# Token mixing's second layer by seven products of half blocks, in four of eight batch elements of a fused attention and mixer kernel

## The chip, the cores and the metric

One core of a Trainium2 chip runs the whole program. The metric is the device time of one execution in microseconds (us), the median of several. All data are 32-bit floats.

## What is computed

For each of 8 batch elements: normalised attention of 12 heads over 448 positions of 64 channels, which gives x of 448 by 768, and then one mixer block on x. Cut to what matters here:

```python
h = np.maximum(xt @ w_tok1, 0.0) @ w_tok2      # xt: 768 x 448, w_tok1: 448 x 256, w_tok2: 256 x 448
u = x + h.transpose(0, 2, 1)                   # token mixing
h2 = np.maximum(u @ w_ch1, 0.0) @ w_ch2        # channel mixing: 768 -> 1536 -> 768
out = u + h2
```

The change concerns the second product of the first of these lines, in each element a matrix of 768 x 256 times one of 256 x 448, whose result is added to x.

## The kernel before

The kernel keeps x and then u of an element as six tiles of 128 channels by 448 positions, `st["uT", b][:, cc]`. The 256 hidden rows of token mixing lie in two tiles `h1` (one for each half of the 256, called jc), each 128 partitions by 768 channels. `tok1` (lines 843 to 877) makes them in two halves of 384 channels (h = 0 and 1), and `tok1_out` (lines 879 to 884) evicts each half with a Relu on ScalarE.

`tok2(b, cc)` (lines 886 to 895) is the second layer for one tile of channels: two matmuls with 448 columns, one for each half of the 256, add up in one PSUM bank (`m_tile`), and VectorE adds the bank to `uT` (line 894). It runs six times per element. After the two tiles t and t + 3, `moving_sums(b, t)` (lines 902 to 914) forms four sums T1 to T4 of quarters of u, two on VectorE and, from the third element on, two on GpSimd.

Channel mixing already uses fewer products than the plain way: `ch1` (line 997) by seven products of half blocks, three times per element, and `ch2` (line 1065) by 15 forms with tables of additions. Both use banks of `ps_M`, of which there are two. Scores of attention and some smaller things use the four banks of `ps_S`. `ch1`'s products i = 0 and 4 are evicted by a ScalarE copy, the others by VectorE (line 1015). Products i = 0, 1 and 5 read u, i = 2, 3, 4 and 6 read T2, T3, T1 and T4 of `moving_sums`.

Attention runs one element ahead, so the attention of element b + 1 lies in between the mixer work of element b. From the third element on (b = 2 to 6) `big_step` makes large blocks of attention and `place` (lines 638 to 655) puts them at written-out places among the mixer items: the first block stands directly behind the last `tok2` and ahead of the first `ch1`. A block brings `beside` items, put directly after it, and `between` items, spread over the mixer items up to the next block. For the first block `beside` is: two scalings of q and k (line 1507), two transposes into `qkT` (line 436, two instructions each), and two additions to the sums of exponentials (line 500).

Every engine runs its instructions in the order in which the program issues them; a list of items with costs (`us(n, cols)`) decides that order, and the costs have no other effect than on order. At the end of an element four finished tiles are transposed into `turned` and the last two are left for the start of the next element, among the items of token mixing (line 1103). SyncE issues nearly all DMAs, among them the weights of channel mixing (`load_units`, up to 7 units of 384 KB ahead) and the q and k of later heads (`loads`), which wait until the tile they overwrite has been transposed.

`raw_pool` has five tiles for the loading of weights, not used any more from the fourth element on. `x_pool` has two tiles that hold the transposed x of an element's two halves. `r_pool` holds scratch tiles r1, r2, r3 and r5 for `ch1` and `ch2`.

Of the kernel before, what the change touches and what calls it, by code (L numbers as in the profile page):

```python
# [8 lines left out]
F32 = mybir.dt.float32  # L9
# [74 lines left out]
def whole(ctx, tc, shifted, pre, q, k, v, g_q, g_k, moe_w_tok1, moe_w_tok2, moe_w_ch1, moe_w_ch2, out):  # L84
# [121 lines left out]
    def raw_tile():  # L206
        return raw_pool.tile([P, WCOLS, 2], U32, name="raw")
# [427 lines left out]
        between += [item(group_sums, t, k) for k in (5, 6)] + loads(n + 3)  # L635
        return [], (6.2, second_block), beside, between

    def place(units, blocks, at):

        res, i, rest = [], 0, []  # L640
        for j, (ahead, block, beside, between) in list(zip(at, blocks)) + [(len(units), ([], None, [], []))]:
            n, done = j - i, 0
            for m in range(n):
                if m == n - 1 and block:
                    res += ahead
                res.append(units[i + m])
                upto = -(-len(rest) * (m + 1) // n)
                res += rest[done:upto]
                done = upto
            if not n:  # L650
                res += rest + ahead
            i, rest = j, between
            if block:
                res += [block] + beside
        return res

# [186 lines left out]
    def tok1(b, jc, h):  # L843

        def main(start, stop):
            for c in range(NM):
                nc.tensor.matmul(  # L847
                    out=st["t1", h][jc][:, 0:HC], lhsT=w1_sb[:, c, jc * P:(jc + 1) * P],
                    rhs=st["x", b, h][:, :, c, :], start=start and c == 0, stop=stop and c == NM - 1)

        def rest(h, starts):
            for i in range(NJ):
                rows = slice(i * D, (i + 1) * D)
                nc.tensor.matmul(  # L854
                    out=st["t1", h][i][:, 0:HC], lhsT=w1_sb[rows, NM, i * P:(i + 1) * P],
                    rhs=st["x", b, h][rows, :, NM, :], start=starts[i], stop=not starts[i])

        alone, first = b > 0 and not shifted, jc == 0
        if first and not (alone and h):
            st["t1", h] = [m_tile() for i in range(NJ)]  # L860
        if not alone:
            main(first, not first)
            if first:
                rest(h, (False, True))
            tok1_out(jc, h)
            return
        if h == 0:
            main(True, False)
            return
        if first:  # L870
            st["t1", h] = [s_tile("t1_ps") for i in range(NJ)]
            rest(0, (False, False))
            rest(1, (True, True))
            for i in range(NJ):
                tok1_out(i, 0)
        main(False, True)
        tok1_out(jc, h)

    def tok1_out(jc, h):

        if h == 0:
            st["h1", jc] = h1_pool.tile([P, C], F32, name="h1", tag="h1")
        nc.scalar.activation(
            out=st["h1", jc][:, h * HC:(h + 1) * HC], in_=st["t1", h][jc][:, 0:HC], func=AF.Relu)

    def tok2(b, cc):
        ps = m_tile()
# [258 lines left out]
    def middle_items(b):  # L1146

        items = []
        for t in range(KC):
            items += [(us(NJ, S), lambda cc=cc: tok2(b, cc)) for cc in (t, KC + t)]  # L1150
            if b:
                items.append((0.0, lambda t=t: moving_sums(b, t)))
        if b == 0:
            return items, [(us(4, S), lambda n=n: first_stage(n)) for n in range(len(stages))]
        items += [(us(6, HS), lambda mp=mp, i=i: ch1(b, mp, i)) for mp in range(KF // 2) for i in range(7)]
        if b == 1:
            double = [(us(6, S), lambda mt=mt, h=h: plain_2(b, mt, h)) for mt in order_2 for h in range(2)]
        else:
            double = [(us(4, HS), lambda f=f, x=x: ch2(b, f, x)) for f in range(NF9) for x in range(2)]
        mixing.update(fn for _, fn in items[3 * KC:] + double)  # L1160
        return items, double
# [91 lines left out]
    for b in range(B):  # L1253
        early, double = middle_items(b)
        if b == 0:
            early, last = first_items(
                tok1_items(0, 0) + x_items(0, 1) + tok1_items(0, 1) + early, double, some)
        else:
            if b > 1 and in_next(b - 1):

                y, z = sends(b - 1, y_order(b - 1)[:4]), left
                left = [y[0], y[1], z[0], y[2], z[1], y[3]]
            run(merge(tok1_items(b, 0), left[:2]))
            begin, early = merge(tok1_items(b, 1) + early[:3 * KC], left[2:]), early[3 * KC:]
            if b == 1 and not shifted:
                run(merge(begin, sums[5:9]))
                early, begin = merge(early[:8], sums[9:]) + early[8:], []
            elif b == 1:
                early, begin = merge(begin + early[:8], sums[5:]) + early[8:], []
            if b == 1:  # L1270
                form_items()
            tail, keep = (4, 2) if b == 1 else (14, 3) if ending(b) else (11, 6)
            last, ends = double[-tail - keep:-tail], double[-tail:]
            double = double[:-tail - keep]
            early = begin + early + double
        lo = (b + AHEAD) * per + 1
        att = []
        if b + AHEAD < B and (shifted or b < 2):
            att = att_items(lo, lo + 10) + x_items(b + AHEAD, 0)
            if shifted:  # L1280
                att += att_items(lo + 10, lo + per)
            elif not b:
                step = att_step(lo + per - 1)
                att += att_items(lo + 10, lo + per - 1) + step[:5] + x_items(1, 1) + step[5:]
            else:
                run(att[:6])
                ahead, block, beside, between = big_step(BIG, False)
                att = att[6:] + att_items(lo + 10, lo + per - 1) + ahead + [block] + beside + between
        elif b + AHEAD < B:
            t = (b + AHEAD) * NPAIR // 2  # L1290
            blocks = [big_step(t + i // 2, i % 2) for i in range(1, NPAIR + 1)]
            blocks[4][3].extend(x_items(b + 1, 0))
            early = place(early, blocks, [near(early, at) for at in BLOCKS])
        if b == 0:
            last = x_items(1, 1) * shifted + merge(last, sums[:5], turns(b, y_order(b)[2:4]))
        else:
            if b + 1 < B:
                last = merge(last, x_items(b + 1, 1))
            last += last_items(b, ends)
        run(merge(att, early) + last)  # L1300
        if b == 0:
            load_units(0)
        left = [] if b and ending(b) else turns(b, y_order(b)[4:])
# [275 lines left out]
```

## Time and profile before

| what | value |
|---|---|
| median of 3 runs | 1277.4 us (1273.76 to 1279.42) |
| the profiled execution's own time | 1277.84 us |
| its span, first to last instruction | 1275.4 us |
| granted TensorE clock, mean | 0.997 |
| period of one element, third to sixth | 148.0, 147.9, 147.9, 147.9 us |
| TensorE busy in each of these | the whole period |
| VectorE, ScalarE, GpSimd busy in the fifth element's period | 92.48, 45.15, 36.61 us |

The page gives for each engine its busy time, share and number of instructions, then the span in 40 slices, then the groups of instructions by source line. A 32-bit matmul appears in the trace as two matmul rows and two weight loads, so the 12 matmuls of one element's second layer are 24 rows of line 889. "PE" is TensorE's matmuls, "PEld" its weight loads, DVE VectorE, ACT ScalarE, POOL GpSimd. Matmuls overlap: the time from one start to the next, not the mean duration of one, tells what they cost.

In the fifth element (b = 4), which the prediction follows, the second layer runs from 726.22 to 735.44 us, the block of attention from 735.44 to 741.61, and the first product of `ch1` starts at 741.61.

### The profile page before, as it was taken

To read this page: it belongs to the slowest core of one execution; us is meant where nothing else is said; L and a number is where in the kernel's file an instruction comes from. 1 tells how busy PE (TensorE), PEld (TensorE's weight loads), DVE (VectorE), ACT (ScalarE), POOL (GpSimd) and SP (SyncE) were. 2 spreads that over 40 slices of the span, in tenths; PEclk is the share of its full clock that TensorE was granted. 3 is DMA by queue.
4 is the path that set the end of the run, shared out by engine and by line. 5 is a ranking of instruction groups with operands and counts; after the bars stand their busy time and mean duration, and the time that the engine had idled before them with its cause. 6 is when DMAs were issued, how large, how long until landed. Compare 5 with 4: busy or idle time off the path is not lost.

```text
span 1275.4 us, 20051 instructions
## 1 busy us (share of the span) xinstructions
PE 1252.2 (98%) x7250; PEld 891.1 (70%) x7250; DVE 796.5 (62%) x1241; ACT 393.9 (31%) x785; POOL 407.0 (32%) x646
## 2 busy tenths in 40 slices
PE   6999999999999999999999999999999999999998
PEld 3444444457645488796778777885787867797998
DVE  6988879756663455855577356765558456554243
ACT  6664433124330134402442044312343024300210
POOL 2310651044994822231223112241122322131222
PEclk9999999999999899999999999999999999999999
DMA  9666687899889686695758767685866864376654
GB/s 204 158 172 174 197 226 188 197 263 253 224 216 260 139 200 162 146 244 110 169 146 188 181 147 181 147 223 121 181 159 150 231 136 139 116 199 145 192 174 105
DMA packets 480272, 228.37 MB, mean 179 GB/s; under 512 B 362900, under 2 KB 440084, under 8 KB 480164
## 3 DMA queue, kind: packets, MB, share of 16 engines
q1 hardware_dynamic: 472626, 211.85, 67.7%
q0 software_dynamic: 4512, 14.46, 3.9%
q8 instruction: 59, 0.97, 0.3%
q10 hardware_dynamic: 3026, 0.69, 0.3%
q14 instruction: 49, 0.40, 0.1%
HBM read 184.26 MB, written 42.66 MB: 178 GB/s over the span
## 4 chain that ended last, share of the span: by engine, by line
PE 88%; DVE 4%; DMA 3%; SPq 1%; ACT 1%; issue 1%; DVEq 0%; ACTq 0%
PE m_ps L1009 26%; PE m_ps L1075 22%; PE s_ps L459 10%; PE o_ps L532 9%; PE m_ps L889 6%; PE m_ps L979 5%; PE m_ps L847 2%; PE t_ps L847 2%; PE m_ps L1058 1%; PE d_ps L512 1%; PE m_ps L512 1%; DMA raw<-wp 1%; DVE stage L383 1%; PE m_ps L854 1%; PE t_ps L433 1%
## 5 line engine op out<-in xcount | busy, mean ns | idle before, releaser
L1075 PE MATMUL m_ps<-hb,unit 128*128 128x224 f32 x1440 | 277.2, 354 | 0.0
L1075 PEld LDWEIGHTS m_ps<-hb,unit 128*128 128x128 f32 x1440 | 270.9, 190 | 8.8 <-issue 7.7
L1009 PE MATMUL m_ps<-tu,unit 128*128 128x224 f32 x1008 | 201.6, 355 | 1.3 <-ACT r L1019 1.3
L1009 PEld LDWEIGHTS m_ps<-tu,unit 128*128 128x128 f32 x1008 | 189.1, 190 | 15.0 <-issue 9.2
L463 ACT ACTIVATE e<-s_ps 128x448 f32<-128x448 f32 x294 | 138.6, 554 | 177.5 <-PE s_ps L459 168.9
L1009 PE MATMUL m_ps<-uT,unit 128*128 128x224 f32 x756 | 151.2, 354 | 0.8 <-DVE hb L1015 0.8
L1009 PEld LDWEIGHTS m_ps<-uT,unit 128*128 128x128 f32 x756 | 142.2, 190 | 7.9 <-issue 4.6
L459 PE MATMUL s_ps<-qkT 64*64 64x448 f32 x1260 | 144.2, 545 | 0.8 <-ACT x L829 0.8
L532 PE MATMUL o_ps<-e,v 64*64 64x448 f32 x1148 | 129.8, 538 | 0.0
L500 DVE TENSOR_TENSOR es<-es,e 128x896 f32<-128x896 f32 x90 | 102.5, 1139 | 13.4 <-ACT e L463 8.4
L1015 DVE TENSOR_TENSOR hb<-m_ps,r 128x448 f32<-128x448 f32 x63 | 39.1, 621 | 106.2 <-POOL r L1015 57.4
L1015 POOL TENSOR_TENSOR hb<-r,r 128x448 f32<-128x448 f32 x21 | 23.9, 1140 | 239.0 <-ACT r L1031 239.0
L459 PEld LDWEIGHTS s_ps<-qkT 64*64 64x64 f32 x1260 | 45.5, 132 | 69.5 <-issue 59.2
L532 PEld LDWEIGHTS o_ps<-e,v 64*64 64x64 f32 x1148 | 45.9, 133 | 61.9 <-issue 59.6
L1486 POOL TENSOR_TENSOR nt<-rs 128x56 f32<-128x56 f32 (+1 forms) x54 | 21.8, 403 | 201.4 <-DVE rs L1478 198.5
L1016 ACT ACTIVATE hb<-hb 128x448 f32<-128x448 f32 x84 | 48.4, 577 | 100.4 <-DVE hb L1015 77.4
L1090 POOL TENSOR_TENSOR uT<-uT,r 128x448 f32<-128x448 f32 x42 | 51.4, 1241 | 78.3 <-DVE r L1090 46.6
L889 PE MATMUL m_ps<-w_sb,h 128*128 128x448 f32 x192 | 75.2, 544 | 0.3 <-DVE uT L894 0.3
L324 POOL TENSOR_TENSOR raw<-raw 128x128 f32<-128x128 f32 x128 | 64.8, 527 | 21.8 <-DMA raw<-wp 17.3
L894 DVE TENSOR_TENSOR uT<-uT,m_ps 128x448 f32<-128x448 f32 x48 | 29.3, 614 | 65.9 <-PE m_ps L889 65.8
L1456 DVE TENSOR_REDUCE ms<-sq 128x28 f32<-128x896 f32 (+2 forms) x44 | 47.4, 1080 | 36.7 <-ACT sq L1443 29.6
L1015 DVE TENSOR_TENSOR r<-m_ps,r 128x448 f32<-128x448 f32 x42 | 26.1, 622 | 64.5 <-PE m_ps L1009 64.5
(153 smaller groups left out, 1626.9 us busy)
## 6 DMA issues: line engine op xcount, KB each, us to landing
unit<-ws SPq DMA_DIRECT2D x267, 384.0 KB, 4.2
raw<-in_moe_w_ch_dram SPq DMA_DIRECT2D x72, 256.0 KB, 3.5
v<-in_v_dram SPq DMA_DIRECT2D x96, 112.0 KB, 3.5
out_dram<-turned SPq DMA_DIRECT2D x182, 56.0 KB, 2.0
xs<-xt SPq DMA_DIRECT2D x52, 168.0 KB, 4.8
qk_t<-in_q_dram SPq DMA_DIRECT2D x144, 56.0 KB, 3.5
qk_t<-in_k_dram SPq DMA_DIRECT2D x144, 56.0 KB, 3.9
x<-xs SPq DMA_DIRECT2D x39, 192.0 KB, 4.0
```

The costliest lines, as they stand in the source:

```text
L324: nc.gpsimd.tensor_tensor(out=at[o], in0=at[x], in1=at[y], op=ALU.add if op == "+" else ALU.subtract)
L459: nc.tensor.matmul(out=pss[i][rows_of(i, a), 0:S], lhsT=qkT[h, 1, k * D:(k + 1) * D], rhs=qkT[h, 0, :], start=True, stop=True)
L463: nc.scalar.activation(out=e[:, i, :], in_=pss[i][:, 0:S], func=AF.Exp)
L500: nc.vector.tensor_tensor(out=es[:], in0=(es if k > 1 else st["e", t, 0])[:], in1=st["e", t, k][:], op=ALU.add)
L532: nc.tensor.matmul(out=st["o", p][a * D:(a + 1) * D, 0:S], lhsT=vt[rows, k * D:(k + 1) * D], rhs=e[rows, :], **kw)
L847: nc.tensor.matmul(out=st["t1", h][jc][:, 0:HC], lhsT=w1_sb[:, c, jc * P:(jc + 1) * P], rhs=st["x", b, h][:, :, c, :], start=start and c = ...
L889: nc.tensor.matmul(out=ps[:, 0:S], lhsT=st["h1", jc][:, cc * P:(cc + 1) * P], rhs=w2_sb[:, jc].rearrange("p c r -> p (c r)"), start=(jc == ...
L979: nc.tensor.matmul(out=ps, lhsT=a[:, o + 2 * half, :], rhs=natural(half * KF + t) if wide else u[:, half * KC + t, :], start=(t == 0 and h ...
L1009: nc.tensor.matmul(out=ps[:, j * HS:(j + 1) * HS], lhsT=w[:, t, j, :], rhs=m, start=(t == 0), stop=(t == KC - 1))
L1015: add = lambda e, o, x, y: e.tensor_tensor(out=o, in0=x, in1=y, op=ALU.add)
L1075: nc.tensor.matmul(out=ps[:, x * HS:(x + 1) * HS], lhsT=st["w"][:, tile_at % 6, :], rhs=hb[:, X_SLOT[f], i, :], start=(i == 0), stop=(i == 3))
L1090: e.tensor_tensor(out=get(out), in0=get(x_), in1=get(y), op=ALU.add if op == "+" else ALU.subtract)
```

## The change

Elements b = 3 to 6 (the fourth to the seventh, `in_seven`) compute the second layer by seven products of half blocks in place of eight. For each pair of channel tiles i and i + 3 the left matrix is cut into two halves of channels by two halves of the 256, the right matrix w_tok2 into two halves of the 256 by two halves of the 448 positions. Each of the seven products is one matmul of 128 x 128 by 128 x 224, with no accumulation in PSUM.

- `right_sums` makes four sums of quarters of w_tok2, once, on VectorE at the end of the third element, in a tile of `raw_pool` that is then kept.
- `left_sums` makes four sums of the halves of `h1` per element, three on VectorE and one on GpSimd, in a tile of `x_pool`. It is called from `tok1` after the two evictions of half h = 1.
- `seven_items` gives nine items in place of six `tok2` and three `moving_sums`. Per pair: a ScalarE copy of product 1 into r; five additions on VectorE (half of u's first tile gets product 5, the second tile gets 4 and 5, r gets 6 and 1, the first tile gets 2 and 3, scratch gets 7); and two additions of 128 x 448 on GpSimd. All three `moving_sums` come after the last of them. Products 1 and 6 share a bank of `ps_S`, 2 and 3 another; 4 and 5 share a bank of `ps_M`; product 7 of pairs 0 and 1 share a bank of `ps_M`.
- `place` gets a flag: with it, the first block's `beside` items are no longer put directly after the block but spread, together with `between`, over the mixer items up to the next block.

```diff
--- before.py
+++ after.py
@@ -635,7 +635,7 @@
         between += [item(group_sums, t, k) for k in (5, 6)] + loads(n + 3)
         return [], (6.2, second_block), beside, between
 
-    def place(units, blocks, at):
+    def place(units, blocks, at, later_beside):
 
         res, i, rest = [], 0, []
         for j, (ahead, block, beside, between) in list(zip(at, blocks)) + [(len(units), ([], None, [], []))]:
@@ -650,7 +650,10 @@
             if not n:
                 res += rest + ahead
             i, rest = j, between
-            if block:
+            if block and later_beside and not j - at[0]:
+                res.append(block)
+                rest = beside + between
+            elif block:
                 res += [block] + beside
         return res
 
@@ -875,6 +878,8 @@
                 tok1_out(i, 0)
         main(False, True)
         tok1_out(jc, h)
+        if in_seven(b):
+            left_sums(jc)
 
     def tok1_out(jc, h):
 
@@ -882,6 +887,89 @@
             st["h1", jc] = h1_pool.tile([P, C], F32, name="h1", tag="h1")
         nc.scalar.activation(
             out=st["h1", jc][:, h * HC:(h + 1) * HC], in_=st["t1", h][jc][:, 0:HC], func=AF.Relu)
+
+    def in_seven(b):
+        return 2 < b < B - 1 and not shifted
+
+    def left_sums(jc):
+
+        A = lambda m, k: st["h1", k][:, m * HC:(m + 1) * HC]
+        if jc == 0:
+            t = x_pool.tile([P, KC, NS, P], F32, name="sums", tag="x")
+            st["S"] = t[:].rearrange("p j c n -> p (j c n)").rearrange("p (q n) -> p q n", q=4)
+            S = st["S"]
+            nc.vector.tensor_tensor(out=S[:, 2], in0=A(0, 0), in1=A(1, 0), op=ALU.subtract)
+            return
+        S = st["S"]
+        nc.vector.tensor_tensor(out=S[:, 0], in0=A(1, 0), in1=A(1, 1), op=ALU.add)
+        nc.vector.tensor_tensor(out=S[:, 1], in0=S[:, 0], in1=A(0, 0), op=ALU.subtract)
+        nc.gpsimd.tensor_tensor(out=S[:, 3], in0=A(0, 1), in1=S[:, 1], op=ALU.subtract)
+
+    def right_sums():
+
+        w2 = w2_sb[:].rearrange("p j c r -> p j (c r)")
+        B = lambda k, n: w2[:, k, n * HS:(n + 1) * HS]
+        t = raw_tile()[:].rearrange("p n w -> p (n w)").bitcast(F32)
+        T1, T2, T3, T4 = (t[:, i * HS:(i + 1) * HS] for i in range(4))
+        nc.vector.tensor_tensor(out=T1, in0=B(0, 1), in1=B(0, 0), op=ALU.subtract)
+        nc.vector.tensor_tensor(out=T2, in0=B(1, 1), in1=T1, op=ALU.subtract)
+        nc.vector.tensor_tensor(out=T3, in0=B(1, 1), in1=B(0, 1), op=ALU.subtract)
+        nc.vector.tensor_tensor(out=T4, in0=B(1, 0), in1=T2, op=ALU.subtract)
+        st["T"] = {1: B(0, 0), 2: B(1, 0), 3: B(1, 1), 4: T4, 5: T1, 6: T2, 7: T3}
+
+    def seven_items(b):
+
+
+        A = lambda m, k: st["h1", k][:, m * HC:(m + 1) * HC]
+        left = {1: lambda: A(0, 0), 2: lambda: A(0, 1), 3: lambda: st["S"][:, 3], 4: lambda: A(1, 1),
+                5: lambda: st["S"][:, 0], 6: lambda: st["S"][:, 1], 7: lambda: st["S"][:, 2]}
+        bank = {1: ("E", 0), 6: ("E", 1), 2: ("D", 0), 3: ("D", 1), 4: ("C", 0), 5: ("C", 1)}
+        add = lambda e, o, x, y: e.tensor_tensor(out=o, in0=x, in1=y, op=ALU.add)
+        half = lambda a, n: a[:, n * HS:(n + 1) * HS]
+
+        def product(q, i):
+            name, n = bank.get(q, ("F%d" % (i // 2), i % 2))
+            key = ("7", name, i if q != 7 else 0)
+            if key not in st:
+                st[key] = s_tile("seven_ps") if name in "DE" else m_tile()
+            out = st["7", q, i] = half(st[key], n)
+            nc.tensor.matmul(
+                out=out, lhsT=left[q]()[:, i * P:(i + 1) * P], rhs=st["T"][q], start=True, stop=True)
+
+        def one(i, qs, last):
+            u1, u2 = st["uT", b][:, i, :], st["uT", b][:, KC + i, :]
+            got = lambda q: st["7", q, i]
+            for q in qs:
+                product(q, i)
+                if q == 1:
+                    st["r", i] = r_tile(i + 1)[:]
+                    nc.scalar.copy(out=half(st["r", i], 0), in_=got(1))
+                if q == 5:
+                    add(nc.vector, half(u1, 1), half(u1, 1), got(5))
+                    add(nc.vector, u2, u2, st["7", "C", i][:, 0:S])
+                if q == 6:
+                    r = st["r", i]
+                    add(nc.vector, half(r, 1), got(6), half(r, 0))
+                if q == 3:
+                    add(nc.vector, u1, u1, st["7", "D", i][:, 0:S])
+                    add(nc.gpsimd, u1, u1, st["r", i])
+            if last:
+                if i % 2 == 0:
+                    st["r3"] = r_tile(1 if i else 5)[:]
+                r3 = half(st["r3"], i % 2)
+                add(nc.vector, r3, got(7), half(st["r", i], 1))
+                both = u2.rearrange("p (n s) -> p n s", n=2)
+                add(nc.gpsimd, both, both, r3.unsqueeze(1).to_broadcast([P, 2, HS]))
+                for k in [k for k in st if k[0] == "7" and k[2] == i and k[1] not in ("F0", "F1")]:
+                    st.pop(k)
+                if i:
+                    st.pop(("7", "F%d" % (i // 2), 0))
+                if i == KC - 1:
+                    for t in range(KC):
+                        moving_sums(b, t)
+        parts = [(0, (2, 1, 4, 7)), (0, (5, 6)), (1, (1, 2)), (0, (3,)), (1, (4, 5, 6)), (1, (3, 7)),
+                 (2, (1, 2, 4)), (2, (5, 6)), (2, (3, 7))]
+        return [(us(len(qs), HS), lambda i=i, qs=qs: one(i, qs, 3 in qs)) for i, qs in parts]
 
     def tok2(b, cc):
         ps = m_tile()
@@ -1150,6 +1238,9 @@
             items += [(us(NJ, S), lambda cc=cc: tok2(b, cc)) for cc in (t, KC + t)]
             if b:
                 items.append((0.0, lambda t=t: moving_sums(b, t)))
+        if in_seven(b):
+            items = seven_items(b)
+            assert len(items) == 3 * KC
         if b == 0:
             return items, [(us(4, S), lambda n=n: first_stage(n)) for n in range(len(stages))]
         items += [(us(6, HS), lambda mp=mp, i=i: ch1(b, mp, i)) for mp in range(KF // 2) for i in range(7)]
@@ -1290,12 +1381,14 @@
             t = (b + AHEAD) * NPAIR // 2
             blocks = [big_step(t + i // 2, i % 2) for i in range(1, NPAIR + 1)]
             blocks[4][3].extend(x_items(b + 1, 0))
-            early = place(early, blocks, [near(early, at) for at in BLOCKS])
+            early = place(early, blocks, [near(early, at) for at in BLOCKS], in_seven(b))
         if b == 0:
             last = x_items(1, 1) * shifted + merge(last, sums[:5], turns(b, y_order(b)[2:4]))
         else:
             if b + 1 < B:
                 last = merge(last, x_items(b + 1, 1))
+            if b == 2 and not shifted:
+                last.append((0.4, right_sums))
             last += last_items(b, ends)
         run(merge(att, early) + last)
         if b == 0:
```

## The prediction

> **What bounds the kernel now.** I read the page first, then the busy times by stretch of the fifth element, then the timelines of TensorE, VectorE and GpSimd there.
>
> ```profile
> PE 1252.2 (98%) x7250; PEld 891.1 (70%) x7250; DVE 796.5 (62%) x1241; ACT 393.9 (31%) x785; POOL 407.0 (32%) x646
> PE 88%; DVE 4%; DMA 3%; SPq 1%; ACT 1%; issue 1%; DVEq 0%; ACTq 0%
> ```
>
> TensorE is busy nearly always, and the chain that ended last is 88% TensorE. So a matmul taken away shortens the span one for one, as long as no other engine becomes late. Three stretches of the fifth element: second layer, attention block, first two products of `ch1` (columns: length, then busy us and instructions of PE, PEld, DVE, ACT, POOL; then clock, DMA):
>
> ```profile
> 726.22:735.44 9.22, 9.22 (x26) 4.29 (x24) 5.53 (x10) 0.49 (x1) 2.80 (x4) 1.00 0.33 53
> 735.44:741.61 6.17, 6.17 (x65) 2.35 (x65) 6.03 (x8) 2.45 (x6) 2.18 (x2) 1.00 0.41 90
> 741.61:746.25 4.64, 4.64 (x28) 4.64 (x25) 2.32 (x4) 3.02 (x6) 0.00 (x0) 1.00 0.78 174
> ```
>
> The first stretch gives the price of the old way: 9.22 us for 24 rows of 448 columns. The third gives the price of the new kind of matmul: 24 rows of 224 columns, each with its own weights, in 4.64 us, 0.193 us a row, 0.386 us a matmul. VectorE has 3.7 us free in the first stretch and almost none in the second. What it does there:
>
> ```profile
> 736.50 0.73 DVE L911 TENSOR_TENSOR tu<-uT,tu 128x224 f32<-128x224 f32 x1
> 737.16 2.55 DVE L1507 TENSOR_TENSOR qk_t<-qk_t,rs 128x896 f32<-128x896 f32 x2
> 739.63 1.16 DVE L436 STREAM_TRANSPOSE qkT<-qk_t 128x448 f32<-128x448 f32 x2
> 740.72 2.24 DVE L500 TENSOR_TENSOR es<-es,e 128x896 f32<-128x896 f32 x2
> 742.87 1.16 DVE L436 STREAM_TRANSPOSE qkT<-qk_t 128x448 f32<-128x448 f32 x2
> 746.52 0.62 DVE L1015 TENSOR_TENSOR hb<-m_ps,r 128x448 f32<-128x448 f32 x1 [2.49 <-PE m_ps L1009]
> ```
>
> The last line matters most: VectorE's first eviction for `ch1` waits 2.49 us for TensorE. That is the slack by which VectorE may be later today. And GpSimd:
>
> ```profile
> 736.25 0.74 POOL L913 TENSOR_TENSOR tu<-uT 128x224 f32<-128x224 f32 x1 [1.38 <-DVE uT L894]
> 737.31 1.45 POOL L914 TENSOR_TENSOR tu<-uT,tu 128x224 f32<-128x224 f32 x1 [0.33 <-DVE tu L911]
> ```
>
> L914 has a median of 0.66 us; here it took 1.45 beside L1507, and L1507 took 2.55 for two that need about 1.08 each alone. L911 takes 0.73 beside GpSimd and 0.39 alone. The two engines hold each other up.
>
> [...] L911, L914 and L1507 stretch, while L894, with one input in PSUM, stays at 0.62 us. [...] 0.384 us at 224 and 0.624 at 448, so I take 0.56 us for the new 384-column sums[...]. [...]
>
> **The change part by part**, in the fifth element.
>
> TensorE. Removed: 24 rows, 9.22 us. Added: 21 matmuls of 0.386, 8.11 us. Difference 1.11 us if TensorE never waits.
>
> What feeds the products (all times as they would lie in the trace of before). Product 4, third in order, wants the last eviction of `h1`, which ends at 726.91; its place is 726.22 + 2 x 0.386 = 726.99. Product 5, at 727.77, wants the sum S0, which VectorE can start at 726.98 and ends at 727.54. Product 6, at 728.15, wants the next sum, 728.10. Product 3, ninth, at 729.31, wants GpSimd's sum: from 728.17, at 1.0 us (between 0.66 at 224 columns and 1.14 at 448), 729.17. All four arrive just in time, two with 0.05 to 0.08 us in hand, which a semaphore's way eats (L894 ends at 730.05, GpSimd's L913 behind it starts at 730.12). I take 0.1 to 0.2 us of waiting together.
>
> Banks. VectorE's additions from 728.3 on run without a gap: a 448-column one every 0.545 us, a 224-column one every 0.31 (its 0.384 less the same 0.075 of overlap), and one transpose 0.58. Product 4 of the second pair needs its bank at 729.7, freed at 729.2; product 7 of the second pair at 731.2, freed at 731.05; product 4 of the third pair at 732.4, freed at 731.95; product 7 at 733.9, freed at 733.2. Another 0 to 0.1 us. TensorE then ends at about 734.5, 0.9 us sooner than before. VectorE's last addition ends at 735.4; the scores want the two last `ps_S` banks at 735.3 and 735.7, freed at 734.6 and 735.1. The three ScalarE copies (0.35 us each, L1019's 0.53 at half the columns) end before ScalarE's next exponential and cost nothing.
>
> Moving sums. GpSimd gets one 1.0 us sum and six additions at 1.14. The last two end at 737.7, being started at 735.4 when VectorE is done. Then six T3 and T4 (0.7), six T1 and T2 on VectorE (0.384[...]), and the two scalings (1.08[...]). [...] VectorE is through at about 743.0 instead of 739.7. `ch1` begins at 734.5 + 6.17 = 740.7 and wants u of the first pairs (GpSimd, 736.5 and 737.7), T2 two products later, 745.3 (done near 740.1), T3 at 747.6 (741.9). All in time.
>
> The moved `beside` items are what makes this hold. As built, VectorE's order is scalings, two transposes, one addition of exponentials, then the eviction of product i = 1, instead of everything first. From 743.0: 1.16 + 1.09 = 745.2, and TensorE delivers at about 745.4. The next eviction, i = 2, ends near 748.8 after another addition and two transposes, and its bank is wanted at 734.5 + 6.17 + 4 x 2.32 = 749.95. Cover 1.1 us. If that is gone, each further us of VectorE is a us of TensorE.
>
> Queues. The q and k of the next heads wait for these transposes, so on SyncE they go some 3 us later, with one more weight unit ahead of them. In before their last landing is near 749.4 for a square (line 1443) at 753.69; after, near 753 for 752.8. ScalarE may wait 0.5 us, and the next exponentials start at 755. Up to seven weight units in advance hide the rest. `right_sums`: four instructions of 0.384 once, at about 552 us, where VectorE is idle 1.85 us and GpSimd's L1049 runs; at worst the eviction after it comes 1.4 us late, and its bank is wanted 3 us later. Nothing. `raw` is last used at 444.5, so keeping a tile costs nothing.
>
> Sum: 1.11 less 0.2 is 0.9 us per element, four elements, 3.6 us. The profiled execution took 1277.84 (span 1275.4 and 2.4 around it) and would take 1274.2. It stands 0.4 over the median, from which I subtract: 1277.4 - 3.6 = 1273.8. The most it can be is 4 x 1.21 (with the one 0.1 us hiccup in the old rows gone too), 1272.6.
>
> **The rivals.**
>
> VectorE paces the stage (0.20). Fifteen additions and three sums are 8.3 us in an 8.1 us stage, where L894 took 3.3. If each hand-over costs 0.1 us more than I count, the bank waits add up to 0.7 us and 0.2 us per element remain: 1276.6. For it: margins of 0.15 us. Against: some have 0.5.
>
> Slower[...] (0.13). If VectorE and GpSimd take turns by whole instructions, from 735.4: 2 x 1.14 + 6 x 0.70 and 6 x 0.384 + 2 x 1.08 are 10.9, VectorE is through near 746.3. The i = 1 eviction ends at 749.2 where 747.6 is wanted, i = 2 another 0.6 late: 2.2 us of TensorE waiting, net +1.3 per element, 1282.5; and each further us of lateness is 4 us. It decides from 1.1 us beyond my 743.0. For it: L914's 1.45. Against: L911's 0.73 is less than 0.74 + 0.38 in turn.
>
> The change doesn't do what it says (0.05): 42 weight loads in place of 24 eat the gain, 9.22/42 = 0.22 us a row, 1277.4. Against: the third stretch, 0.193 with a load for each.
>
> **How the numbers follow.** All hidden 0.62, at 1273.8. About 0.5% is what a measurement of this kernel can tell from no change, 1271.0 to 1283.8; even the whole gain is under that, so "within" has most. Faster by more, 0.09, is the first case with the spread of the runs (5.7 us over three). Slower by more, 0.07, is half of the third, with lateness 0.3 us beyond the figure there. The range goes from 1271.0 to 1279.5: below it 0.09, above it 0.11, nearly all of the slower case.
>
> **What would show it.** The second layer's first to last product takes 8.1 to 8.4 us, and the attention block behind it still 6.2. Period of elements four to six near 147.0. TensorE's waits in these periods stay under 0.3 us. Wrong if waits of `seven_ps` or `m_ps` matmuls on VectorE exceed 0.5 us an element, if `ch1` waits for u or T, or if the periods don't shrink.

## The result, and the profile after

The changed kernel took 1268.99 us (median of seven runs, 1267.1 to 1272.23), the kernel before 1277.4 us (seven runs, 1273.76 to 1280.09): a ratio of 0.9949 with a 95% interval of 0.9929 to 0.997. A second comparison (experiment `again`, below) gave 0.9967, 0.9953 to 0.998. The profiled execution after took 1268.99 us, its span is 1267.2 us. The forecast was 1273.8 us with a range from 1271.0: the time lies below the range.

The page of the changed kernel, busy times and the chain that ended last:

```profile
PE 1244.7 (98%) x7322; PEld 903.5 (71%) x7322; DVE 827.8 (65%) x1293; ACT 397.1 (31%) x797; POOL 434.0 (34%) x674
PE 86%; DVE 5%; SPq 3%; DMA 2%; issue 1%; ACT 1%; POOL 1%; DVEq 0%; ACTq 0%; POOLq 0%
```

TensorE is as full as before and busy for 7.5 us less, though it has 72 instructions more (4 x 18). Not all of the 7.5 us is work that went away: 3.4 us of it is a stretch of half clock in the profile of before, shown below. VectorE has 31 us more and GpSimd 27 us more, both beside it. The three stretches of the fifth element that were shown of before (second layer, attention block, first two products of `ch1`):

```profile
720.95:729.19 8.24, 8.24 (x44) 7.58 (x42) 6.68 (x16) 1.53 (x4) 4.64 (x5) 1.00 0.62 97
729.19:735.37 6.18, 6.18 (x65) 2.49 (x64) 5.87 (x9) 2.45 (x6) 6.11 (x7) 1.00 0.55 150
735.37:740.00 4.63, 4.63 (x28) 4.63 (x25) 4.63 (x6) 1.99 (x5) 2.37 (x3) 1.00 0.00 0
```

The second layer takes 8.24 us in place of 9.22, the block behind it the same 6.18. The 42 products alone are 8.11, so TensorE waits 0.13 us in the stage. VectorE now works through all three stretches: 6.68 of 8.24, 5.87 of 6.18, 4.63 of 4.63.

The fourth to the seventh element, each from its first product to that of the next (columns as before). After:

```profile
574.03:720.95 146.92, 146.92 (x928) 118.66 (x926) 98.83 (x148) 46.20 (x95) 44.73 (x65) 1.00 0.70 168
720.95:867.87 146.92, 146.92 (x928) 118.67 (x927) 98.87 (x148) 46.20 (x95) 44.73 (x65) 1.00 0.69 168
867.87:1014.79 146.92, 146.92 (x928) 118.68 (x927) 98.76 (x148) 46.19 (x95) 44.70 (x65) 1.00 0.70 169
1014.79:1159.16 144.37, 144.37 (x903) 117.92 (x902) 86.28 (x131) 36.81 (x75) 38.12 (x41) 1.00 0.63 159
sum 585.13, PE 585.13 PEld 473.94 DVE 382.74 ACT 175.40 POOL 172.28; mean PE 146.28 PEld 118.48 DVE 95.68 ACT 43.85 POOL 43.07
```

The same elements before, one of them and the sum:

```profile
726.22:874.10 147.88, 147.88 (x910) 115.25 (x908) 92.48 (x136) 45.15 (x92) 36.61 (x58) 1.00 0.69 167
...
sum 589.02, PE 589.02 PEld 460.72 DVE 357.75 ACT 171.47 POOL 139.76; mean PE 147.25 PEld 115.18 DVE 89.44 ACT 42.87 POOL 34.94
```

The difference is 3.89 us, all that the change does to these elements. In the fifth element the second layer alone is 0.98 us shorter and the period 0.96, so the move of the `beside` items gains nothing by itself; it only keeps the gain (`beside`, below). But the two profiled executions are 8.85 us apart. Of the rest, 3.63 us lie between the start of the second layer in the second element and in the third (168.93 us before, 165.30 after), 0.79 in the elements ahead of that, 0.59 outside the span, and nothing elsewhere (the third element is 0.10 longer, what follows 0.06 shorter). None of the changed instructions runs so early: `right_sums`, the first of them, runs at 548 us. TensorE's timeline of before shows where the 3.63 are:

```profile
421.27 2.31 PE L854 MATMUL t_ps<-x,w_sb 64*128 64x384 f32 x4 [1.38 <-DMA x<-xs]
423.51 6.92 PE L847 MATMUL t_ps<-x,w_sb 128*128 128x384 f32 x12
```

The same two lines of code in an execution of the kernel before that kept its clock (`control`):

```profile
419.94 1.33 PE L854 MATMUL t_ps<-x,w_sb 64*128 64x384 f32 x4
421.20 4.14 PE L847 MATMUL t_ps<-x,w_sb 128*128 128x384 f32 x12
```

Twelve rows that take 4.14 us took 6.92. The granted clock of that stretch of before says why (the third number from the end is the clock):

```profile
420.00:430.00 10.00, 8.73 (x16) 4.25 (x17) 0.00 (x0) 1.28 (x3) 9.45 (x21) 0.66 0.79 157
```

From 422.3 us the clock stood at 0.5 for 6.8 us, which costs 3.4 us. In the profile after it was 1.00 there, though TensorE waited 1.54 us for the same x. In the nine traces in which the clock held there (a mean of 0.999 or 1.000 in each), this part, from the second element to the third, still takes anything from 162.8 (`beside`) to 167.2 us (`vector`); TensorE's waits for the transfer of x alone lie between 0 and 2.1 us in them.

Such stretches are not of this kernel alone: the profile of before has one, those of `five` and `last` (below) two each, with mean clocks of 0.997, 0.996 and 0.996. A mean clock of 0.998 or less goes in the runs of this study with medians that are 1 to 6 us longer: the profiled execution of before was one of these, at 0.997, and of the seven after six had 1.000 and one, the 1272.23, 0.998.

### The profile page after: what moved, and what is told of

Read it like the earlier page. It is cut to its first block, busy times and chain, and to the rows that moved or that the text cites. A ratio compares the mean times of both kernels' runs of the same rounds, so it can differ in the third digit from the quotient of the medians.

```text
span 1267.2 us, 20382 instructions
## 1 busy us (share of the span) xinstructions
PE 1244.7 (98%) x7322; PEld 903.5 (71%) x7322; DVE 827.8 (65%) x1293; ACT 397.1 (31%) x797; POOL 434.0 (34%) x674
## 4 chain that ended last, share of the span: by engine, by line
PE 86%; DVE 5%; SPq 3%; DMA 2%; issue 1%; ACT 1%; POOL 1%; DVEq 0%; ACTq 0%; POOLq 0%
PE m_ps L1097 26%; PE m_ps L1163 22%; PE s_ps L459 10%; PE o_ps L532 9%; PE m_ps L1067 5%; PE m_ps L977 3%; PE m_ps L850 3%; PE t_ps L850 2%; PE m_ps L1146 1%; PE seven_ps L936 1%; PE d_ps L512 1%; PE m_ps L936 1%; PE m_ps L512 1%; DVE es L500 1%; DMA xs<-xt 1%
## 5 line engine op out<-in xcount | busy, mean ns | idle before, releaser
L532 PE MATMUL o_ps<-e,v 64*64 64x448 f32 x1148 | 130.0, 538 | 0.0
L1103 POOL TENSOR_TENSOR hb<-r,r 128x448 f32<-128x448 f32 x21 | 23.8, 1133 | 217.5 <-ACT r L1119 217.5
L1103 DVE TENSOR_TENSOR hb<-m_ps,r 128x448 f32<-128x448 f32 x63 | 39.1, 620 | 88.9 <-POOL r L1103 57.5
L532 PEld LDWEIGHTS o_ps<-e,v 64*64 64x64 f32 x1148 | 46.1, 133 | 61.9 <-issue 59.8
L324 POOL TENSOR_TENSOR raw<-raw 128x128 f32<-128x128 f32 x128 | 65.4, 531 | 20.8 <-DMA raw<-wp 16.3
L1103 DVE TENSOR_TENSOR r<-m_ps,r 128x448 f32<-128x448 f32 x42 | 26.0, 618 | 55.2 <-PE m_ps L1097 55.2
L1174 ACT COPY r<-m_ps 128x448 f32<-128x448 f32 x24 | 12.8, 532 | 156.5 <-PE m_ps L1163 156.5
L1178 DVE TENSOR_TENSOR uT<-uT,m_ps 128x448 f32<-128x448 f32 x41 | 24.9, 619 | 54.8 <-PE m_ps L1163 54.8
```

Source lines behind the costliest of these rows:

```text
L324: nc.gpsimd.tensor_tensor(out=at[o], in0=at[x], in1=at[y], op=ALU.add if op == "+" else ALU.subtract)
L532: nc.tensor.matmul(out=st["o", p][a * D:(a + 1) * D, 0:S], lhsT=vt[rows, k * D:(k + 1) * D], rhs=e[rows, :], **kw)
L1103: add = lambda e, o, x, y: e.tensor_tensor(out=o, in0=x, in1=y, op=ALU.add)
L1178: e.tensor_tensor(out=get(out), in0=get(x_), in1=get(y), op=ALU.add if op == "+" else ALU.subtract)
```

## The experiments

**Theory A**: the change is worth 3.9 us, and the rest of the 8.4 us between the medians comes from stretches at half clock that runs of before happened to have. **Theory B**: the change also does away with the clock's fall, so that all of the 8.4 us are its own.

### control: the kernel before, unchanged, against itself

> The kernel before, unchanged. Theory A (chance): the change's own worth is about 3.9 us, and what the medians differ by beyond that is a stretch of half granted clock of 6.8 us near 422 us, in front of every changed instruction, that comes in some executions of either kernel and costs 3.4 us. Then the control's ratio is 1.00, and its executions fall into two groups, clock 1.000 and near 1274 us, clock 0.997 and near 1278 us. Theory B (the change does it): a clock of 0.997 is the kernel before's own, all executions of the control show it, and none is under 1276 us.

Measured: 1272.49 us (22 runs) against 1273.43 (53 runs), ratio 1.0002, 0.9992 to 1.0012. Its profile shows a clock of 1.00 from 0 to 430 us and in the four elements (573 to 1162 us), 162.89 us from the second element to the third, and 588.98 us for the four elements (589.02 above). The 75 runs, put together by their mean clock:

| clock | runs of `control`: median | runs of before: median |
|---|---|---|
| 1.000 | 6: 1273.1 | 21: 1272.3 |
| 0.999 | 12: 1271.7 | 18: 1272.8 |
| 0.998 | 3: 1276.0 | 13: 1275.1 |
| 0.997 | 1: 1277.5 | 1: 1278.1 |

So the unchanged kernel takes 1272 to 1273 us where the clock holds, 4 to 5 us less than the median that the forecast started from. (A mean of 0.999 is less than a fall like that of before, whose 6.8 us at half clock make 0.997.) A holds in the main, though its two groups near 1274 and 1278 did not come out: only 2 of the 75 runs were at 0.997 and 16 at 0.998. B, which wanted every run at 0.997 and above 1276, falls.

These 75 runs were all on one chip. On the two chips of the later experiments the kernel before has medians of 1276.84 and 1274.44 us (19 runs each), with 8 and 7 runs at 0.998 or less; at 1.000 it takes 1273.0 on both. So a median near 1277 is what enough falls make of a kernel of 1273. Nor does the change keep the clock up: of the runs of after that stood beside those 7 of 19, 4 of 14 had 0.998 or less (`again`).

### fill_before and fill_after: what makes the clock fall

The 1.4 us wait for x stood just ahead of the fall, so each kernel was given six matmuls to do in it, on a tile that is rewritten afterwards (b = 2 only):

```diff
             rest(0, (False, False))
+            if b == 2:
+                for _ in range(6):
+                    nc.tensor.matmul(
+                        out=st["t1", h][0][:, 0:P], lhsT=ident[:, :], rhs=ident[:, :], start=True, stop=True)
             rest(1, (True, True))
```

> The kernel before, with six identity matmuls (1.3 us) put in front of the third element's first matmul on the x that arrives late, so that TensorE is busy while it waits; they write a bank that is overwritten afterwards. Theory A, that the clock falls because TensorE stands still there: clock 1.000 in every execution, near 1274 us, ratio to the kernel before 0.998 (the mean of its two groups), narrow spread. Rival, that the clock falls for another reason: clock 0.997 stays in as many executions as before, ratio 1.00 or 0.1% above.

> The changed kernel with the same six matmuls. Theory A: near 1268.5 us as the changed kernel without a clock stretch, clock 1.000 in every execution, 4 to 6 us under the kernel before with the six matmuls: the pair of both is the change without the clock's chance, and should differ by 3.9 us. If they differ by 6 us or more, the change gives more outside of its four elements than the profile shows.

Measured: before with the filling 1273.24 us (14 runs, ratio 1.0003, 0.9994 to 1.0012), after with it 1268.94 us (8 runs, ratio 0.9967, 0.9956 to 0.9979). The pair is 4.3 us apart, near the 3.9 of A. On the cause of the fall they say little. If standing still for x were all of it, before with the filling should have come to a ratio of 0.998 and kept a clock of 1.000 throughout; it did neither. Clocks of 0.998 or less came in 2 of 22 runs with the filling (2 of 14 before, 0 of 8 after) and in 18 of 75 of before without. And `extra4`, below, waited 2.00 us for x at this place and kept its clock at 1.00. The length of the wait alone does not decide. What else does is open (more on it at the end).

### again: the comparison made a second time

> The changed kernel, unchanged, against runs of the kernel before on the same chip at the same time. If the change is worth what the periods of its four elements say, 3.9 us, the ratio is 0.9970 (1273.4 to 1269.5 at the earlier chip's level), with its executions spread by the granted clock as those of the kernel before are. If the first comparison's 0.9949 was the change, it comes again.

Measured: 1270.86 us (14 runs, 1265.88 to 1274.37) against 1274.44 (19 runs), ratio 0.9967, 0.9953 to 0.998. At a clock of 0.999 the medians are 1270.0 and 1274.3, at 1.000 they are 1271.1 and 1273.0, of four to seven runs each. The four elements take 585.14 us in its trace. The 3.89 us of the trace are 0.9969 of 1273.4, so the trace, this run and `fill_after` agree to 0.0002, and the first comparison holds that value at the edge of its interval.

### beside: the move of the `beside` items taken back

```diff
-            early = place(early, blocks, [near(early, at) for at in BLOCKS], in_seven(b))
+            early = place(early, blocks, [near(early, at) for at in BLOCKS], False)
```

> The changed kernel with the first block's items directly behind the block again, as before the change. If their move is what keeps VectorE in time: the scalings end 17.7 us after the first product as now, then four transposes and two additions (4.5 us) come ahead of the eviction of product i = 1 of the channel mixing, which ends 22.9 us after the first product where its bank is wanted at 21.4: about 1.4 us of TensorE waiting in each of four elements, 5.6 us more than the changed kernel, 1274 to 1275 us, the gain gone. Rival, that VectorE has slack enough: the same time as the changed kernel, period of an element 146.9 us.

Measured: 1275.41 us (22 runs), ratio 1.0017, 1.0006 to 1.0028. The stage still takes 8.24, but the periods are 148.3 to 148.6, 1.4 to 1.7 more than after, and the sum of the four elements is 591.08. The whole gain is gone, and 2 us more. ScalarE's timeline of `beside`, and TensorE's:

```profile
738.89 0.67 ACT L439 ACTIVATE qkT<-qkT,g_t 128x448 f32<-128x448 f32 x1 [3.17 <-DVE qkT L436]
739.47 0.51 ACT L1107 COPY r<-m_ps 128x448 f32<-128x448 f32 x1
```

```profile
734.47 4.81 PE L1097 MATMUL m_ps<-uT,unit 128*128 128x224 f32 x24
740.03 7.46 PE L1097 MATMUL m_ps<-tu,unit 128*128 128x224 f32 x36 [0.76 <-ACT r L1107]
```

And ScalarE's of after:

```profile
738.02 0.53 ACT L1107 COPY r<-m_ps 128x448 f32<-128x448 f32 x1 [1.40 <-PE m_ps L1097]
739.80 0.67 ACT L439 ACTIVATE qkT<-qkT,g_t 128x448 f32<-128x448 f32 x1 [1.25 <-DVE qkT L436]
```

The first wait is not VectorE's own. With the items directly after the block, ScalarE's scaling of q and k (L439) stands ahead of its copy of `ch1`'s first product (L1107). L439 waits 3.17 us for VectorE's transposes, which stand behind the late scalings (734.76 to 737.77), and the copy that frees a bank of `ps_M` waits behind it. In after the copy goes first, the moment TensorE delivers. TensorE loses 0.92 us here (740.03 where 24 rows after 734.47 would have let it go on at 739.1) and 0.49 more inside the next 36 rows (7.46 us where after takes 6.97): that one is VectorE's, whose first eviction ends at 742.61 in `beside`. The 1.4 us that I expected came, but for the larger part on another engine than I had it.

### extra2 and extra4: how much later VectorE may be

Two or four more additions of 128 x 384 on VectorE, right after the moving sums, into scratch that nobody reads later:

```diff
                     for t in range(KC):
                         moving_sums(b, t)
+                    spare = st["S"][:, 0]
+                    for _ in range(4):
+                        nc.vector.tensor_tensor(out=spare, in0=spare, in1=st["S"][:, 1], op=ALU.add)
```

> As the kernel with four more additions on VectorE, with two. They make VectorE some 1.0 us later. Four cost 1.58 us per element, so that 0.4 us of some 2.0 were covered, or each costs more than I took. If the cover is 0.4 us, two cost 0.6 us, period 147.5; if it is 0.8, two cost 0.2 to 0.3, period 147.2.

> The changed kernel with four more additions of 128 x 384 on VectorE in each of the four elements, behind the moving sums and ahead of the scalings; their result is used by nothing. They make VectorE some 2.0 us later. If the cover is what the trace of the changed kernel shows (the eviction of product i = 2 ends at 743.87 where its bank is wanted at 744.65, 0.8 us), TensorE waits 1.2 us per element and the period becomes 148.1 us. If VectorE has much more slack than that, the period stays 146.9[...].

Measured, one execution each: 1274.86 and 1275.27 us; what counts are the periods in the traces, 147.33 to 147.53 with two and 148.50 to 148.54 with four, against 146.92. VectorE in `extra4`:

```profile
737.24 3.13 DVE L972 TENSOR_TENSOR sums<-sums 128x384 f32<-128x384 f32 x4
740.29 2.09 DVE L1603 TENSOR_TENSOR qk_t<-qk_t,rs 128x896 f32<-128x896 f32 x2
```

Four additions cost 3.13 us, but the scalings behind them fall to 2.09 from 3.01 (at its shortest L1507 takes 1.08 in before): in after GpSimd's last sum ends 16.8 us after the first product, and these scalings start 17.8 after it. So in the fifth element the eviction of product i = 2 comes 2.16 us later, not 3.1; with two it comes 0.95 later. From the first product of `ch1` over its first 60 rows TensorE takes 13.08 us with four (736.90 to 749.98), 11.88 with two (739.77 to 751.65) and 11.46 in after (735.37 to 746.83), so it pays 1.62 and 0.42 there. Between the two cases that is 1.20 us for 1.21 us; drawn back to zero, about 0.5 us are free. The periods, which grow by 1.58 to 1.62 and by 0.41 to 0.61, put it at 0.4 to 0.5. The cover of 0.8 that I read from the trace was too large, and with it the 148.1 that I expected of four too low.

### vector: GpSimd's six additions on VectorE

```diff
-                    add(nc.gpsimd, u1, u1, st["r", i])
+                    add(nc.vector, u1, u1, st["r", i])
...
-                add(nc.gpsimd, both, both, r3.unsqueeze(1).to_broadcast([P, 2, HS]))
+                add(nc.vector, both, both, r3.unsqueeze(1).to_broadcast([P, 2, HS]))
```

> The changed kernel with GpSimd's six additions to u per element done by VectorE. VectorE gets 6 x 0.55 = 3.3 us more inside the second layer, GpSimd loses 6.8 us, and moving sums need not take turns with those additions. If the pace of VectorE in the stage decides, as the rival in the prediction has it, the banks come free later, about 1.1 us per pair: the second layer takes 9.5 to 10.5 us instead of 8.24, period 148 to 149. [...]

Measured, one execution: 1278.95 us; stage 9.33 (expected 9.5 to 10.5), block 7.03, period 148.85, 1.93 more than after. TensorE's timeline:

```profile
730.56 0.65 PE L936 MATMUL m_ps<-raw,sums 128*128 128x224 f32 x2 [0.19 <-DVE r L927]
...
732.14 0.62 PE L936 MATMUL m_ps<-raw,h 128*128 128x224 f32 x2 [0.17 <-DVE uT L927]
...
736.02 0.98 PE L459 MATMUL s_ps<-qkT 64*64 64x448 f32 x8 [0.63 <-ACT e L463]
```

This is the first rival come true: VectorE paces the stage, products wait for banks that its additions free, and the scores of the block behind it wait too. The six additions on GpSimd are what keeps the stage at 8.24.

### last: the eighth element too

```diff
-        return 2 < b < B - 1 and not shifted
+        return 2 < b and not shifted
```

> The changed kernel with the seven products in the eighth element too, behind whose second layer no block of attention stands. Theory (the block is the cover): the second layer takes 8.24 us instead of 9.12, but the first product of the channel mixing waits for GpSimd's additions to u, which end 10.2 us after the first product in the fifth element: about 1.2 to 1.5 us of waiting, so that the last element is not shorter, and up to 0.5 us longer, than in the changed kernel (108.0 us from its first product of the second layer to the end). Rival (the saving is the matmuls' whatever stands behind): 107.0 us.

Measured, one execution: 1277.24 us with two stretches at half clock, at 309 and 428 us, so only the eighth element counts here. From its first product to the end it takes 108.48 us, where after takes 108.00. The stage saves the same 0.9 (8.28 us against 9.12), and then:

```profile
1177.06 4.05 PE L1097 MATMUL m_ps<-uT,unit 128*128 128x224 f32 x20 [1.01 <-POOL uT L927]
```

There is no attention block behind the second layer of this element. `ch1` comes at once and waits for GpSimd's additions. The 6.18 us of the block are the cover under which GpSimd and VectorE finish in the other elements.

### five: the third element too, with `right_sums` made in the second

```diff
-        return 2 < b < B - 1 and not shifted
+        return 1 < b < B - 1 and not shifted
...
-            if b == 2 and not shifted:
+            if b == 1 and not shifted:
```

> The changed kernel with the seven products in the third element as well, the right sums made at the end of the second. The third element also has a block of attention behind its second layer, so the theory gives one more saving of 0.97 us, period of the third element 146.9 to 147.2 instead of 147.8 to 148.2, total 1 us under the changed kernel. Rival: the tile kept from the five of the weights' pool makes loads and sums for the second layer of channel mixing later, which go on until 444 us, and SyncE stands: the same time as the changed kernel or slower by some us.

Measured: 1277.14 us (14 runs) against 1276.84 (19 runs), ratio 1.001, 0.9995 to 1.0025: the gain of the other four elements is gone. The third element takes 154.75 us in its trace, 6.6 more than in after, where it is computed the old way; the fourth to the sixth take 146.9 to 147.2. TensorE, then GpSimd, in the third element of `five`:

```profile
443.45 1.02 PE L1097 MATMUL m_ps<-uT,unit 128*128 128x224 f32 x4
448.18 4.03 PE L1097 MATMUL m_ps<-uT,unit 128*128 128x224 f32 x11 [3.70 <-POOL uT L927]
```

```profile
437.97 2.12 POOL L324 TENSOR_TENSOR raw<-raw 128x128 f32<-128x128 f32 x4
440.05 2.22 POOL L927 TENSOR_TENSOR uT<-uT,r 128x448 f32<-128x448 f32 x2
442.23 2.11 POOL L324 TENSOR_TENSOR raw<-raw 128x128 f32<-128x128 f32 x4
...
446.99 2.22 POOL L927 TENSOR_TENSOR uT<-uT,r 128x448 f32<-128x448 f32 x2
```

The raw tile was not what stands in the way of an earlier start, as the rival had it: GpSimd works without a pause from 431 us on and waits for no tile. Its queue is: until 447 us it makes and sends the weight forms for the elements to come (L324 and the like), and the additions to u stand between them. The last two begin 18 us after the first product, in after 9 us after it.

This wait is not all of the 6.6 us. Behind it the next 20 rows take 5.57 us from start to start (448.18 to 453.75) where 0.193 us a row makes 3.86, and the mean clock of the element is 0.99, of the next 1.00: 1.7 us more, which fits a stretch at half clock. A second wait of TensorE, which ends at 457.83, takes 1.64. Of the 14 runs 11 had a clock of 0.998 or less, against 8 of the 19 of before. Whether the waits of the third element bring these falls is not shown: the other fall of this trace, near 308 us (four rows of L532 take 2.51 us there, 0.92 just ahead), comes ahead of everything that was changed.

## Why the prediction was wrong, step by step

**Right: the size of the change.** The forecast was 0.9 us per element and 3.6 in all; the traces show 0.96 to 1.01 and 3.89. The stage was to take 8.1 to 8.4 (8.24), the block 6.2 (6.18), the periods near 147.0 (146.92), waits under 0.3 (0.13). The four products said to come just in time do: product 6 starts 2.02 us after the first product, where its undisturbed place is 1.93, product 3 at 3.23 where it is 3.09. The price of a row, 0.193 us, held, and so did the 0.56 us for the sums of 384 columns, an estimate between 0.384 at 224 columns and 0.624 at 448 (measured 0.56).

**Wrong: the time from which it was subtracted.** "It stands 0.4 over the median, from which I subtract: 1277.4 - 3.6 = 1273.8." The sum was made against an execution in which half clock cost 3.4 us, and the median of three runs seemed to confirm it. Its mean clock of 0.997 stood beside the time, and matmuls of L847 that took 6.92 us for twelve rows stood in the trace. That is the step that failed, the first term of the sum: 1277.4 is not what the kernel takes where the clock holds. Medians of 1272.3 to 1273.1 are, on three chips (`control` and the runs of before beside the later experiments). From there the same sum gives 1268.7 to 1269.5; after took 1268.99. That the seven runs of the first comparison were held up in this way is shown for the profiled one alone; of the others no clock is on record, and it is argued from the 75 runs of `control`'s table and from the chip on which the median was 1276.84. What the waits for x added to the base is open.

**Wrong with it: the lower end.** The range went down only to 1271.0 for "the spread of the runs (5.7 us over three)". Three runs spread by 5.7 us are no base known to 0.4 us; the case of the likely gain from 1273.76, the fastest of the three, was 1270.2 and belonged inside. "The most it can be is 4 x 1.21" was right for the change (3.89 of 4.84) and wrong for the difference of two medians.

**Right in kind, off in size: VectorE's lateness.** VectorE in the fifth element of after (5.27 us earlier than in before; L998 and L999 are moving sums, L1600 the scalings, L1103 evictions of `ch1`):

```profile
729.83 0.39 DVE L927 TENSOR_TENSOR r<-m_ps,r 128x224 f32<-128x224 f32 x1
730.13 1.31 DVE L998 TENSOR_TENSOR tu<-uT 128x224 f32<-128x224 f32 x1
731.54 1.14 DVE L999 TENSOR_TENSOR tu<-uT,tu 128x224 f32<-128x224 f32 x1
732.61 0.84 DVE L998 TENSOR_TENSOR tu<-uT 128x224 f32<-128x224 f32 x1
...
735.68 3.01 DVE L1600 TENSOR_TENSOR qk_t<-qk_t,rs 128x896 f32<-128x896 f32 x2
738.61 1.16 DVE L436 STREAM_TRANSPOSE qkT<-qk_t 128x448 f32<-128x448 f32 x2
739.70 1.04 DVE L500 TENSOR_TENSOR es<-es,e 128x896 f32<-128x896 f32 x1
740.67 0.61 DVE L1103 TENSOR_TENSOR hb<-m_ps,r 128x448 f32<-128x448 f32 x1
...
743.28 0.58 DVE L1103 TENSOR_TENSOR r<-m_ps,r 128x448 f32<-128x448 f32 x1
```

Its last addition ends at 730.22, which is 735.5 on the clock of before (forecast 735.4). From there sums and scalings take until 738.69, 743.96 in place of the forecast "about 743.0": 8.5 us where I reckoned 7.4. (The 7.4 takes only a part of each instruction as holding the other engine up. How large that part is was an estimate of mine, and no run shows it.) The eviction of i = 2 ends at 743.86, its bank is wanted at 735.37 + 4 x 2.32 = 744.65: 0.8 us, not 1.1, and by `extra2` and `extra4` only 0.4 to 0.5 of it can be used. "Each further us of VectorE is a us of TensorE" was right: 1.20 for 1.21. The rival of turns by whole instructions, which "decides from 1.1 us beyond my 743.0", was thus 0.4 to 0.5 us away. VectorE was 1.0 us later than reckoned and the gain came whole all the same; that is in part luck.

**The step that was incomplete: what the moved `beside` items do.** I gave VectorE's order alone as the reason. `beside` shows the larger half on ScalarE, whose copy of `ch1`'s first product must not stand behind work that waits for the late scalings. The price, 1.4 to 1.7 us an element, exceeds what the whole change is worth.

**The rivals.** VectorE did not pace the stage as built; it does with six more additions (`vector`). (The 8.3 us that the prediction gives for fifteen additions and three sums has the transpose of 0.58 in it; without it they are 7.7 at the same prices.) The 42 weight loads cost nothing that shows: 42 rows with a load each take 8.24 us, 0.196 a row with the 0.13 of waiting in it, against 0.193 in before. `right_sums` was hidden: VectorE's next eviction starts at 551.39, behind the last of its sums, and TensorE runs on without a wait from 545 to 574 us. The queues moved past on SyncE left no wait of TensorE in these elements.

No version tried beats the one as built.

## What to carry to other kernels

Before a sum is subtracted from a median, check the granted clock of the profiled execution: look for matmuls of one line and form that take longer in one place (here 6.92 us for twelve rows in place of 4.14, at a clock of 0.5); what they cost, here 3.4 us, comes off the base. When work is added to an engine that has slack, ask of every other engine what stands in order behind something that waits for it; here a copy on ScalarE cost TensorE 0.92 us and VectorE's own eviction 0.49. When a product scheme moves work from TensorE to VectorE and GpSimd, look for a stretch of other TensorE work behind it in which they can finish: here it won 0.96 us with 6.18 us of attention behind it, and nothing in `last`, without (108.48 us against 108.00).

## What the runs showed of the hardware

In the fifth element of after VectorE's additions with both inputs in SBUF and GpSimd's hold each other up and go one for one. GpSimd's side:

```profile
725.55 6.89 POOL L927 TENSOR_TENSOR uT<-uT,r 128x448 f32<-128x448 f32 x6 [1.60 <-DVE uT L927]
732.39 0.81 POOL L1001 TENSOR_TENSOR tu<-uT 128x224 f32<-128x224 f32 x1
733.16 0.81 POOL L1002 TENSOR_TENSOR tu<-uT,tu 128x224 f32<-128x224 f32 x1
```

While GpSimd adds 448 columns, one addition of 224 columns on VectorE with both inputs in SBUF, 0.38 us at its shortest (L916 and L917 in after), takes 1.31 and 1.14. Those with one input in PSUM keep their time in the same stretch: 0.38 at 224 columns, 0.61 at 448 (729.00 and 729.30 us). When GpSimd comes to 224 columns, one of its additions starts every 0.77 us and VectorE's start in pairs every 1.53. One after the other, 0.66 (the median of L914 in before) and 0.38 would be 1.04, not 0.77: the two overlap in part, and whole instructions in turn, with which the rival came to 10.9 us, are too much for the 8.5 measured.

One for one is not a rule, though. In `five` an addition of VectorE stood through a row of GpSimd's:

```profile
448.16 3.74 DVE L998 TENSOR_TENSOR tu<-uT 128x224 f32<-128x224 f32 x1 [5.08 <-POOL uT L927]
```

```profile
449.16 0.66 POOL L1001 TENSOR_TENSOR tu<-uT 128x224 f32<-128x224 f32 x1
...
451.00 0.65 POOL L1002 TENSOR_TENSOR tu<-uT,tu 128x224 f32<-128x224 f32 x1
```

GpSimd did four of 224 columns, one every 0.61 us (0.77 in after), and VectorE's one, started ahead of them, ended 0.25 us behind the last. What decides whose turn it is these runs do not show.

Four falls of the clock lasted about 3.4 us or twice that. In before it stood at 0.50 from 422.32 to 429.15 us, 6.83 us. In `last` its mean was 0.62 from 308 to 317 us and 0.72 from 427 to 433; with a clock of 0.50 as in before, that is an estimate of 6.8 and 3.4 us. In the third element of `five` the 1.71 us lost are 3.4 us at the same clock. TensorE had waited ahead of each fall: 1.38 us in before, 1.84 and 0.69 + 0.20 us in `last`, 1.52 and 3.70 us in `five`. But the clock stayed at 1.00 behind waits of 1.54 us in after, 2.00 us in `extra4` and 1.70 us in `control` (at 212 us). So the length of the wait alone does not decide here, and what does is not shown.
